# Seeding a partial sum from ScalarE, and folding the 64-channel rest into the seven products: 49 matmuls a chunk for 50

## The chip, the core and the metric

The kernel runs on one core of a Trainium2 chip. Its engines are named as the profile names them: PE is TensorE (matmuls; PEld is its weight load), DVE is VectorE, ACT is ScalarE, POOL is GpSimd, SP is SyncE, which here only issues transfers. Each engine takes its own instructions in the order built, and waits for others through semaphores. The metric is the device time of one execution in microseconds (us); the median of three runs of the kernel before is 1569.44 us.

## What is computed

One pre-norm transformer block over x of 2048 tokens by 576 channels, in fp32. The second half, the gated MLP, matters here:

```python
h = x + _A_ref(_layernorm(x, axis=-1), A_wqkv, A_wo)       # sliding dilated attention, 32 heads
...
g = jnp.einsum("bsd,df->bsf", x, w_gate)                   # x is _layernorm(h); D 576, F 4608
u = jnp.einsum("bsd,df->bsf", x, w_up)
h = _sigmoid(g) * u
return jnp.einsum("bsf,fd->bsd", h, w_down)
```

## The kernel before

**Precision.** A product in fp32 is made of three fp32r passes: each operand is split into a high part (ACT copies and rounds it) and a low part (DVE subtracts the high part), and high x high, high x low and low x high are accumulated in PSUM. `split` (L104 on ACT, L105 on DVE) does this for all operands.

**Channels.** Of the 576 input channels 512 are four slabs of 128; the last 64, the rest, lie twice on 128 partitions (high part above, low part below), so that two matmuls (`rest`, L754) make its three passes.

**Tokens and chunks.** The 2048 tokens are four blocks of 512. F is worked in 36 chunks of 128. The program's loop over `c` has 84 items: 12 plain chunks on block 0 (`single`), 24 paired chunks on blocks 0 and 1 (`pair`), 12 plain chunks that give block 1 its first third of F, and 36 paired chunks on blocks 2 and 3, the last pair (c from 48 on). Attention of the later blocks, its output projection, and the preparation of the next pair's operands run as background generators (`under_first`, `under_rest`) under these chunks.

**A paired chunk** multiplies a 2 by 2 block matrix of activations (a00 and a01: two pairs of channel slabs of one block; a10, a11 of the other) with a 2 by 2 block of weights (gate and up) in Strassen-Winograd form: seven products (weights b00, b10, t2, t3, t1, t4, b11; operands a00, a01, s2, s3, s1, a11, s4) of two slabs in three passes, so six matmuls each (`prod`, L747), and four rests of two matmuls: 50 matmuls of 128x128 by 512. The products accumulate in three PSUM banks, `b_tile`: b1 takes b00, then t2, then t1, then b11, and is copied out or added between them; b2 takes b10; b3 takes t3 and t4. Sums of banks are made by copying a bank to an `s` tile (ACT: L824, L834, L838), adding another bank to it (DVE: L829, L843, L848), then a sigmoid (ACT: L830, L849) and the gating product (DVE).

```python
        prod(b1, X["a00"], w, "b00", True)
        act.activation(s1, b1, AF.Copy)
        prod(b2, X["a01"], w, "b10", True)
        added[0] = dve.tensor_tensor(s1, s1, b2, ALU.add)
        act.activation(s1, s1, AF.Sigmoid)
```

`turn` rotates the banks by one from chunk to chunk. A plain chunk has its gate in the first bank and its up half in the second.

**The down product.** Between the products stand small units of down-projection matmuls (128x128 by 288, six to a unit in the last pair, PSUM tile `dp`, two buffers). In the last pair they are in the same seven-product form over two chunks (`seven`, `down_seven`): 14 units for two chunks, in each half k = 0 to 6 in two buffers, where k = 0, 2, 4, 6 accumulate in one buffer and 1, 3 and 5 in the other. After each unit ACT copies the buffer to an `ev` tile (L936; two units to a tile, four tiles), and POOL issues an accumulating DMA of it to DRAM (L939).

**Weights.** SP loads a chunk's weights two chunks ahead (`wg`, 640 KB in the last pair). `weights` makes the sums t1 to t4 in a tile `tw` (DVE, L727, L728, L730) and splits all into w1 (two buffers), w2, w3 and w4 (one buffer each). 

**Order.** A list scheduler sets each engine's order from priorities (`high_priority`: 700 for what empties banks, 400 for weights and operand splits) and from its own estimate of when things are ready.

## Time and profile before

| | |
|---|---|
| median of three runs | 1569.44 us (1568.37 to 1570.96) |
| span of the profiled execution, first to last instruction | 1566.1 us |
| PE, PEld busy | 1545.8 us (99%), 1374.2 us (88%) |
| DVE, ACT, POOL busy | 1254.3 us (80%), 882.6 us (56%), 207.4 us (13%) |
| granted TensorE clock | 1.000 |
| the last pair (936.6 us to the end) | 629.5 us |

The profile lists one execution, whose span is 3.3 us shorter than the median of the timed runs; a run's time has a little around the span. Busy shares are means over stages with different limits, so the stages are looked at one by one: attention with the first projections up to 219 us, the first plain chunks up to 350 us, the first pair up to 773.6 us, the second row of plain chunks up to 936.6 us, the last pair from there. In a group's row stand line, engine, operation, tiles, count, then busy time, mean ns of one, and idle time before. In the rows of windows stand the window, its length, busy us of PE, PEld, DVE, ACT, POOL with counts, clock, DMA share and GB/s.

### The profile page before, as it was taken

The page shows a single profiled execution, that of the slowest core. Times are in us where ns is not written, and L with a number is a line of the kernel's source. Part 1 is how long each engine was busy: PE and PEld are TensorE (multiplying, and loading weights), DVE is VectorE, ACT ScalarE, POOL GpSimd, SP SyncE. Part 2 cuts the span into 40 slices and gives each one's busy share as a digit, 9 for nine tenths or more (in the row PEclk, how much of TensorE's full clock was granted, in tenths as well). Part 3 has the DMA queues.
Part 4 walks back from the last instruction along what each step waited for, and adds up shares of the span by engine and source line. Part 5 has one row for each costly group of instructions (what it writes and reads, how often), then busy time and mean ns, then how long its engine had stood idle before and what let it go on. Part 6 is the DMA issues. An engine that isn't in the chain of part 4 may idle for free.

```text
span 1566.1 us, 22356 instructions
## 1 busy us (share of the span) xinstructions
PE 1545.8 (99%) x8520; PEld 1374.2 (88%) x8520; DVE 1254.3 (80%) x1880; ACT 882.6 (56%) x1584; POOL 207.4 (13%) x252
## 2 busy tenths in 40 slices
PE   8999999999999999999999999999999999999998
PEld 7999988887888888888888988888888888888888
DVE  7998999979999999999536688866777776677754
ACT  6632344435566555665542355766777666677761
POOL 3300000011000010000101000121112112112212
PEclk9999999999999999999999999999999999999999
DMA  8646555366565775665683424998899989989983
GB/s 281 219 166 222 190 200 183 107 225 199 145 174 150 200 183 150 162 159 125 180 243 113 179 85 119 205 180 176 170 181 186 172 172 183 175 170 181 185 166 137
DMA packets 77148, 273.96 MB, mean 175 GB/s; under 512 B 8336, under 2 KB 14224, under 8 KB 76144
## 3 DMA queue, kind: packets, MB, share of 16 engines
q0 software_dynamic: 28192, 107.29, 37.4%
q1 hardware_dynamic: 41216, 145.11, 27.8%
q10 hardware_dynamic: 7632, 20.12, 3.3%
q8 instruction: 66, 1.08, 0.3%
q14 instruction: 42, 0.34, 0.1%
HBM read 143.98 MB, written 130.87 MB: 176 GB/s over the span
## 4 chain that ended last, share of the span: by engine, by line
PE 82%; DVE 10%; DMA 5%; ACT 2%; issue 1%; POOL 0%; SPq 0%; ACTq 0%; POOLq 0%; DVEq 0%
PE b L747 40%; PE dp L868 14%; PE dp L930 11%; PE b L754 8%; PE acc L157 4%; DMA wg<-in_wmlp_dram 2%; DVE pr L189 2%; DVE lg L193 1%; DVE pr L215 1%; PE b L157 1%; PE bgp L157 1%; DMA x<-tok 1%; DVE w L105 1%; DMA kw<-k 1%; DVE pr L221 1%
## 5 line engine op out<-in xcount | busy, mean ns | idle before, releaser
L747 PE MATMUL b<-tl,w 128*128 128x512 f32 x1692 | 429.6, 393 | 1.2 <-ACT s L824 0.6
L747 PEld LDWEIGHTS b<-tl,w 128*128 128x128 f32 x1692 | 305.8, 188 | 57.9 <-ACT tl L104 1.2
L747 PE MATMUL b<-th,w 128*128 128x512 f32 x1332 | 343.0, 392 | 0.5 <-DVE s L843 0.5
L747 PEld LDWEIGHTS b<-th,w 128*128 128x128 f32 x1332 | 242.7, 188 | 45.3 <-DVE s L843 0.9
L936 ACT ACTIVATE ev<-dp 128x576 f32<-128x576 f32 x224 | 145.0, 647 | 62.9 <-PE dp L930 58.6
L754 PE MATMUL b<-th,w 128*128 128x512 f32 x564 | 174.9, 391 | 0.0
L939 POOL DMA_DIRECT2D h<-ev x128 | 109.2, 853 | 459.4 <-ACT ev L936 445.6
L104 ACT ACTIVATE w<-wg 128x384 fp32r<-128x384 f32 (+1 forms) x186 | 111.0, 600 | 98.5 <-PE b L754 54.4
L157 PE MATMUL acc<-qw,th 128*128 128x432 f32 x512 | 154.5, 363 | 2.4 <-DVE th L109 2.3
L105 DVE TENSOR_TENSOR w<-wg,w 128x384 fp32r<-128x384 f32 (+1 forms) x186 | 121.0, 656 | 36.7 <-ACT w L104 36.5
L105 DVE TENSOR_TENSOR w<-tw,w 128x512 fp32r<-128x512 f32 x120 | 82.6, 688 | 81.6 <-ACT w L104 80.7
L754 PEld LDWEIGHTS b<-th,w 128*128 128x128 f32 x564 | 106.0, 188 | 23.0
L868 PE MATMUL dp<-d,h1h 128*128 128x288 f32 x640 | 118.8, 295 | 0.0
L868 PE MATMUL dp<-d,h0h 128*128 128x288 f32 x608 | 112.2, 295 | 0.0
L876 ACT ACTIVATE stage<-dp 128x576 f32<-128x576 f32 x104 | 66.9, 646 | 68.1 <-PE dp L868 67.8
L157 PEld LDWEIGHTS acc<-qw,th 128*128 128x128 f32 x512 | 96.9, 189 | 7.7 <-DVE th L109 3.1
L868 PEld LDWEIGHTS dp<-d,h1h 128*128 128x128 f32 x640 | 98.7, 189 | 3.0
L868 PEld LDWEIGHTS dp<-d,h0h 128*128 128x128 f32 x608 | 94.0, 189 | 3.5 <-DVE stage L878 0.3
L104 ACT ACTIVATE w<-tw 128x512 fp32r<-128x512 f32 x120 | 75.3, 628 | 35.7 <-PE b L747 34.6
L157 PE MATMUL acc<-qw,tl 128*128 128x432 f32 x256 | 92.8, 363 | 0.1
L189 DVE TENSOR_TENSOR pr<-kw,q 128x2304 f32<-128x2304 f32 x32 | 81.8, 2555 | 8.3 <-DMA kw<-k 8.1
L884 POOL DMA_DIRECT2D h<-stage x26 | 31.1, 1197 | 416.2 <-ACT stage L876 337.2
(323 smaller groups left out, 2969.6 us busy)
## 6 DMA issues: line engine op xcount, KB each, us to landing
h<-ev POOLq DMA_DIRECT2D x96, 576.0 KB, 7.3
wg<-in_wmlp_dram SPq DMA_DIRECT2D x47, 928.0 KB, 5.2
h<-stage POOLq DMA_DIRECT2D x26, 1152.0 KB, 11.6
wg<-in_wmlp_dram SPq DMA_DIRECT2D x36, 640.0 KB, 4.2
kw<-k SPq DMA_DIRECT2D x16, 792.0 KB, 4.6
vw<-v SPq DMA_DIRECT2D x16, 792.0 KB, 4.9
wd<-in_wmlp_dram SPq DMA_DIRECT2D x18, 576.0 KB, 7.2
h<-ev POOLq DMA_DIRECT2D x32, 288.0 KB, 6.8
```

What stands on the lines that cost most here:

```text
L104: act.activation(hi, src, AF.Copy)
L105: splits.append(dve.tensor_tensor(lo, src, f32(hi), ALU.subtract))
L157: pe.matmul(ps[:, :n], a[:, c, js], m[:, c], start=k == 0, stop=False)
L189: dve.tensor_tensor(pr, both(kw, u), q[:, us].unsqueeze(2).broadcast_to([P, 2, W, CG]), ALU.mult)
L747: pe.matmul(ps, wt[:, a, k0 + c], xx[:, m + c], start=first and k == 0, stop=k == 5, skip_group_check=True)
L754: pe.matmul(ps, wt[:, a, k0], xx[:, 4], start=False, stop=a == 1, skip_group_check=True)
L868: pe.matmul(ps[:, i, :DH2], a[:, js], d[:, m, i * DH2:(i + 1) * DH2], start=k == 0, stop=k == n)
L876: act.activation(hv, ps, AF.Copy)
L884: pool.dma_start(hacc[b], hs, accum_op=ALU.add, max_dma_last_dim=8 * D)
L930: pe.matmul(ps[:, i, :DH2], a[x][:, js], m[y], start=k in (0, 1, 3) and q == 0, stop=q == 2, skip_group_check=True)
L936: act.activation(hs[:, k % 2], ps[:, :, :DH2], AF.Copy)
L939: pool.dma_start(hsev[:, u, k0:k + 1], hs[:, :k + 1 - k0], accum_op=ALU.add, max_dma_last_dim=8 * D)
```

## The change

**Seeding.** In `pair`, from the second chunk of a row on, ACT copies the first product from its bank into the bank of b10 (PSUM to PSUM) rather than to s1, b10 accumulates on it, and the sigmoid reads the bank: the DVE sum L829 goes. The products' order becomes b00, t3, t2, b10, t1, t4, b11. The banks no longer rotate: the first two swap from chunk to chunk, the third stays with t3 and t4. At the start of a row the first bank is the second one of `b_tile`, in which the plain chunk before has its up half. The gating product of the second block is issued ahead of b11.

**Rest in the products.** For the last pair the rest is halved into 32 channels for each column block of operands and laid out on four 32-partition quarters: operand high, low, high, low against weight high, high, low, low. One matmul makes all passes, and the halves take part in the seven sums: 7 x 7 = 49 matmuls. For this, `proj_scr` writes the raw rest of blocks 2 and 3 to DRAM, 16 POOL transfers read it back fourfold, `sums_rest` adds four DVE sums, and `split_quads` splits each of the seven operands with one ACT copy and two DVE subtractions, where three operands had one subtraction. The weights come from another array (768 KB a chunk for 640), are summed in place in `wg` after b00, b10 and b11 have been split from it, and take 10 DVE and 5 ACT instructions for 7 and 4.

**Space.** `s` has 3 buffers for 4, `ev` 3 for 4, `d3` 1 for 2.

```diff
+
+    def split_quads(t, src):
+        act.activation(t, src, AF.Copy)
+        for q in (32, 96):
+            dve.tensor_tensor(t[q:q + 32], src[q:q + 32], f32(t[q:q + 32]), ALU.subtract)
...
-        dve.tensor_tensor(rd, a0[:, 4], a1[:, 4], ALU.subtract)
-        yield
+        if rd is not None:
+            dve.tensor_tensor(rd, a0[:, 4], a1[:, 4], ALU.subtract)
+            yield
+    def sums_rest(q0, q1, s1):
+        (a00, a01), (a10, a11) = q0, q1
+        dve.tensor_tensor(s1, a10, a11, ALU.add)
+        yield
+        dve.tensor_tensor(a10, a00, a10, ALU.subtract)
+        yield
+        dve.tensor_tensor(a00, s1, a00, ALU.subtract)
+        yield
+        dve.tensor_tensor(a01, a01, a00, ALU.subtract)
+        yield
+        return dict(s1=s1, s2=a00, s3=a10, s4=a01, a11=a11)
+
+
+    def x_full(n, raw, rest):
+        if n in ("a01", "a11", "s4"):
+            t = th_tile()
+            r = t[:, 4]
+        else:
+            t = tl_tile()
+            r = xr.tile([P, TB], F32R, name="x" + n)
+        split(t[:, 0:2], t[:, 2:4], raw)
+        split_quads(r, rest)
+        XR[n] = r
+        return t
+
+    XR = {}
+    xr = None
...
-    def weights(kind, ws, down):
+    def full_weights(ws):
+        r = ws[:, :GF].rearrange("p (b c n) -> p b c n", b=4, c=3)
+        r1 = r.rearrange("p b c n -> p (b c) n")
+
+        def quads(t, src):
+            act.activation(t, src, AF.Copy)
+            dve.tensor_tensor(t[64:128], src[64:128], f32(t[64:128]), ALU.subtract)
+
+        with tc.high_priority(HI):
+            w1 = gw.tile([P, 2, 5, P], F32R, bufs=2, name="w1")
+            act.activation(w1[:, :, 0:3], r[:, 2:4], AF.Copy)
+            dve.tensor_tensor(w1[:, :, 3:5], r[:, 2:4, 1:3], f32(w1[:, :, 1:3]), ALU.subtract)
+            dve.tensor_tensor(w1[64:128, :, 0], r[64:128, 2:4, 0], f32(w1[64:128, :, 0]),
+                              ALU.subtract)
+            w4 = gw.tile([P, 6, P], F32R, name="w4")
+            act.activation(w4[:, 0:3], r[:, 0], AF.Copy)
+            dve.tensor_tensor(w4[:, 3:5], r[:, 0, 1:3], f32(w4[:, 1:3]), ALU.subtract)
+            dve.tensor_tensor(w4[64:128, 0], r[64:128, 0, 0], f32(w4[64:128, 0]), ALU.subtract)
+            dve.tensor_tensor(r1[:, 0:6], r1[:, 0:6], r1[:, 3:9], ALU.subtract)
+            dve.tensor_tensor(r[:, 2], r[:, 0], r[:, 2], ALU.add)
+            dve.tensor_tensor(r[:, 3], r[:, 3], r[:, 2], ALU.subtract)
+            ts = []
+            for name, b in (("w2", 0), ("w3", 2)):
+                t = gw.tile([P, 2, 4, P], F32R, name=name)
+                split(t[:, :, 0:2], t[:, :, 2:4], r[:, b:b + 2, 1:3])
+                ts += [t[:, 0], t[:, 1]]
+            tr = gw.tile([P, 8, P], F32R, tag="tw", name="tr")
+            quads(tr[:, 0:4], r[:, :, 0])
+        ww = {n: (t[:, 1:5], t[:, 0]) for n, t in
+              (("b00", w1[:, 0]), ("b10", w1[:, 1]), ("b11", w4))}
+        ww.update({n: (t, tr[:, i]) for i, (n, t) in enumerate(zip(("t3", "t1", "t2", "t4"), ts))})
+        return ww, None
+
+    def weights(kind, ws):
...
         k = 0
         for c in range(2):
             for a, m in ((0, 0), (0, 2), (1, 0)):
-                pe.matmul(ps, wt[:, a, k0 + c], xx[:, m + c], start=first and k == 0,
+                lhs = wt[:, a, k0 + c] if isinstance(k0, int) else wt[:, 2 * a + c]
+                pe.matmul(ps, lhs, xx[:, m + c], start=first and k == 0,
                           stop=k == 5, skip_group_check=True)
                 k += 1
+
+    def product(ps, n, xn, w, first, rests):
+        prod(ps, X[xn], w, n, first)
+        if isinstance(w[n][1], int):
+            for m, wn in rests:
+                rest(ps, X[m], w, wn)
+        else:
+            pe.matmul(ps, w[n][1], XR[xn], start=False, stop=True, skip_group_check=True)
 
     def rest(ps, xx, w, n):
         wt, k0 = w[n]
...
-        return gh.tile([P, TB], F32, tag="s", bufs=4, name="s")
+        return gh.tile([P, TB], F32, tag="s", bufs=3, name="s")
...
     added = [None]
     gated = [None]
 
-    turn = [2]
-
-    def pair(X, w, between, last):
-        turn[0] += 1
-        b1, b2, b3 = (b_tile(turn[0] + k) for k in range(3))
+    order = [1, 0, 2]
+
+    def pair(w, between, last):
+        n1, n2, n3 = order[:3]
+        clean = order[3:]
+        order[:] = [n2, n1, n3, True]
+        b1, b3, b2 = b_tile(n1), b_tile(n3), b_tile(n2)
         s1, s2, s3 = s_tile(), s_tile(), s_tile()
-        prod(b1, X["a00"], w, "b00", True)
+        product(b1, "b00", "a00", w, True, ())
         with tc.high_priority(HC):
-            act.activation(s1, b1, AF.Copy)
+            act.activation(b2 if clean else s1, b1, AF.Copy)
         between(0)
-        prod(b2, X["a01"], w, "b10", True)
-        rest(b2, X["a01"], w, "g4")
+        product(b3, "t3", "s3", w, True, ())
         with tc.high_priority(HC):
-            added[0] = dve.tensor_tensor(s1, s1, b2, ALU.add)
-            act.activation(s1, s1, AF.Sigmoid)
+            act.activation(s3, b3, AF.Copy)
         between(1)
-        prod(b1, X["s2"], w, "t2", False)
+        product(b1, "t2", "s2", w, False, ())
         with tc.high_priority(HC):
             act.activation(s2, b1, AF.Copy)
         between(2)
-        prod(b3, X["s3"], w, "t3", True)
+        product(b2, "b10", "a01", w, not clean, (("a01", "g4"),))
         with tc.high_priority(HC):
-            act.activation(s3, b3, AF.Copy)
+            if clean:
+                act.activation(s1, b2, AF.Sigmoid)
+            else:
+                dve.tensor_tensor(s1, s1, b2, ALU.add)
+                act.activation(s1, s1, AF.Sigmoid)
         between(3)
-        prod(b1, X["s1"], w, "t1", False)
-        rest(b1, X["a11"], w, "u4")
+        product(b1, "t1", "s1", w, False, (("a11", "u4"),))
         with tc.high_priority(HC):
             added[0] = dve.tensor_tensor(s3, s3, b1, ALU.add)
         between(4)
-        prod(b3, X["a11"], w, "t4", False)
-        rest(b3, X["a11"], w, "g4")
+        product(b3, "t4", "a11", w, False, (("a11", "g4"),))
         with tc.high_priority(HC):
             added[0] = dve.tensor_tensor(s2, s2, b3, ALU.add)
             gated[0] = act.activation(s2, s2, AF.Sigmoid)
         between(5)
-        prod(b1, X["s4"], w, "b11", False)
-        rest(b1, X["s4"], w, "u4")
         with tc.high_priority(HC):
-            last((s1, b1), (s2, s3))
+            last(1, s2, s3)
+        product(b1, "b11", "s4", w, False, (("s4", "u4"),))
+        with tc.high_priority(HC):
+            last(0, s1, b1)
         between(6)
 
     tails = {}
...
-                    hs = st.tile([P, 2, 2, DH2], F32, bufs=4, name="ev")
+                    hs = st.tile([P, 2, 2, DH2], F32, bufs=3, name="ev")
...
+        elif b > 1:
+            pool.dma_start(rscr[b - 2], raw[0:DR, 4])
...
         s = [pp.tile([P, 2, TB], F32, name=f"rs{i}") for i in range(3)]
         rd = pp.tile([P, TB], F32, name="rd")
         if p == 1:
+            rr = [[pp.tile([P, TB], F32, name=f"rr{i}{h}") for h in range(2)] for i in range(2)]
+            for i in range(2):
+                for h in range(2):
+                    a = rscr[i][32 * h:32 * h + 32, :]
+                    for q in range(4):
+                        pool.dma_start(rr[i][h][32 * q:32 * q + 32], a)
+                    yield
             for n in ("a00", "a01"):
                 a = a0[:, 0:2] if n == "a00" else a0[:, 2:4]
                 with tc.high_priority(HI):
-                    Xn[n] = x_half(a, None if n == "a00" else a0[:, 4])
+                    Xn[n] = x_full(n, a, rr[0][n == "a01"])
                 yield
-        raw = yield from sums(a0, a1, a1[:, 0:2] if p == 1 else a0[:, 0:2], *s, rd)
+            raw = yield from sums(a0, a1, a1[:, 0:2], *s, None)
+            rq = yield from sums_rest(*rr, rd)
+            raw = {n: (raw[n][0], rq[n]) for n in rq}
+            for n in names:
+                with tc.high_priority(HI):
+                    Xn[n] = x_full(n, *raw[n])
+                yield
+            return raw
+        raw = yield from sums(a0, a1, a0[:, 0:2], *s, rd)
         for n in names:
             with tc.high_priority(HI):
                 Xn[n] = x_half(*raw[n])
...
+        if c in (NSTD, NF + NSTD):
+            del order[3:]
-                    Xn[n] = x_half(*raw[n])
+                    Xn[n] = x_full(n, *raw[n])
-            wc = weights(items[c + 1][0], wg, c + 1 < NF + NSTD)
+            wc = (full_weights(wg) if c + 1 >= NF + NSTD else
+                  weights(items[c + 1][0], wg))
-            wg = load_gu(items[c + 2][2], n=WC if c + 2 < NF + NSTD else GU)
+            wg = load_gu(items[c + 2][2], c + 2 >= NF + NSTD)
-        def last(h0, h1):
-            hid[0] = hidden(*h0, "h0")
-            hid[1] = hidden(*h1, "h1")
+        def last(t, sg, ps):
+            hid[t] = hidden(sg, ps, f"h{t}")
...
```

What this does to the order is shown at three places; b1 to b3 are the three banks, `dp` the down units, w1 to w4 weights, `tr` the rests of the weights (new), `xa..`, `xs..` those of the operands (new).

PE, end of the first chunk of the last pair (c = 48), before: t1 and its rest, t4, b11, then the next chunk's b00 and b10, t2, t3, then the first unit of the down products (h0).

```order
L747 MATMUL b2_9212<-tl_9019,w3_9036 128x512 x6
L754 MATMUL b2_9212<-th_9022,w4_9034 128x512 x2
L747 MATMUL b1_9214<-th_9022,w3_9036 128x512 x6
L754 MATMUL b1_9214<-th_9022,w1_9031 128x512 x2
L747 MATMUL b2_9212<-th_8904,w4_9034 128x512 x6
L754 MATMUL b2_9212<-th_8904,w4_9034 128x512 x2
L747 MATMUL b3_9345<-tl_8832,w1_9194 128x512 x6
L747 MATMUL b1_9346<-th_8835,w1_9194 128x512 x6
L754 MATMUL b1_9346<-th_8835,w1_9194 128x512 x2
L747 MATMUL b3_9345<-tl_8892,w2_9198 128x512 x6
L747 MATMUL b2_9347<-tl_8895,w2_9198 128x512 x6
L930 MATMUL dp_9382<-d_9230,h0h_9188 128x288
```

The same place now: the next chunk's b00 has moved up ahead of t4, its rest matmul is the first row; t1 stands behind t4, b11 directly behind t1, and the first matmul of the h0 unit directly behind b11.

```order
L825 MATMUL b1_9249<-xa00_8860,w1_9061 128x512
L825 MATMUL b3_9084<-xs3_8985,tr_8954 128x512
L815 MATMUL b3_9084<-th_9051,w3_8951 128x512 x6
L825 MATMUL b3_9084<-th_9051,tr_8954 128x512
L825 MATMUL b2_9083<-xs2_8968,tr_8954 128x512
L815 MATMUL b2_9083<-tl_9044,w2_8948 128x512 x6
L825 MATMUL b2_9083<-xs1_9045,tr_8954 128x512
L815 MATMUL b2_9083<-th_8991,w4_8941 128x512 x6
L825 MATMUL b2_9083<-th_8991,w4_8941 128x512
L1009 MATMUL dp_9422<-d_9268,h0h_9223 128x288
L815 MATMUL b2_9251<-th_8876,w1_9061 128x512 x5
L815 MATMUL b3_9250<-tl_8984,w2_9072 128x512 x2
```

PE in the steady part of the last pair, around the units s1, h1 and s4 (the fifth to the seventh of a half), before: between any two units stands a product.

```order
L930 MATMUL dp<-d,s1h 128x288 x2
L930 MATMUL dp<-d,s1l 128x288
L930 MATMUL dp<-d,s1h 128x288
L747 MATMUL b_12066<-th,w_11854 128x512 x6
L754 MATMUL b_12066<-th,w_11854 128x512 x2
L930 MATMUL dp<-d,h1h 128x288
L930 MATMUL dp<-d,h1l 128x288
L930 MATMUL dp<-d,h1h 128x288 x2
L930 MATMUL dp<-d,h1l 128x288
L930 MATMUL dp<-d,h1h 128x288
L747 MATMUL b_12065<-tl,w_11858 128x512 x6
L930 MATMUL dp<-d_11552,s4h 128x288
```

Now s1, h1 and s4 follow each other between b00 and t3, with nothing between.

```order
L1009 MATMUL dp<-d,s1h 128x288 x2
L1009 MATMUL dp<-d,s1l 128x288
L1009 MATMUL dp<-d,s1h 128x288
L1009 MATMUL dp<-d,h1h 128x288
L1009 MATMUL dp<-d,h1l 128x288
L1009 MATMUL dp<-d,h1h 128x288 x2
L1009 MATMUL dp<-d,h1l 128x288
L1009 MATMUL dp<-d,h1h 128x288
L1009 MATMUL dp<-d_11965,s4h 128x288
L1009 MATMUL dp<-d_11965,s4l 128x288
L1009 MATMUL dp<-d_11965,s4h 128x288 x2
L815 MATMUL b_12484<-tl,w_12277 128x512 x2
```

DVE in the steady part, from the gating product behind b11 (its bank as input) on, before: w4's split (384 wide), and the sums L728 and L730 in their own tile `tw`, which do not wait for it.

```order
L1187 TENSOR_TENSOR r_12180<-s,b_12065 128x512
L105 TENSOR_TENSOR w_12050<-wg,w_12050 128x384
L728 TENSOR_TENSOR tw<-wg,tw 128x256
L105 TENSOR_TENSOR h0l<-r_12180,h0h 128x512
L730 TENSOR_TENSOR tw<-wg,tw 128x256
L829 TENSOR_TENSOR s<-s,b_12216 128x512
L105 TENSOR_TENSOR w_12201<-tw,w_12201 128x512
L843 TENSOR_TENSOR s<-s,b_12215 128x512
```

Now the split of w4 (L764, L765), whose single buffer b11 was the last to read, the three in-place sums (L766 to L768) and the splits of w2, w3 and the rests stand in one row behind it, all of them for the next chunk's t3 and t2.

```order
L1285 TENSOR_TENSOR r_9821<-s,b_9706 128x512
L764 TENSOR_TENSOR w_9688<-wg,w_9688 128x256
L765 TENSOR_TENSOR w_9688<-wg,w_9688 64x128
L1276 TENSOR_TENSOR wd<-wd 128x288
L107 TENSOR_TENSOR h0l<-r_9821,h0h 128x512
L766 TENSOR_TENSOR wg<-wg 128x768
L767 TENSOR_TENSOR wg<-wg 128x384
L768 TENSOR_TENSOR wg<-wg 128x384
L107 TENSOR_TENSOR w_9695<-wg,w_9695 128x2x256
L107 TENSOR_TENSOR w_9698<-wg,w_9698 128x2x256
L754 TENSOR_TENSOR tr<-wg,tr 64x512
L922 TENSOR_TENSOR s<-s,b_9859 128x512
```

46 lines of the change are left out of this document (27 added, 19 removed).

## The prediction

> **What bounds the kernel now.** I read the shares first, then windows by stage, then the groups and the row of single instructions in the stage that the change is for.
>
> ```profile
> PE 1545.8 (99%) x8520; PEld 1374.2 (88%) x8520; DVE 1254.3 (80%) x1880; ACT 882.6 (56%) x1584; POOL 207.4 (13%) x252
> core 0: us, PE busy (x) PEld busy (x) DVE busy (x) ACT busy (x) POOL busy (x), PEclk, DMA share, GB/s
> 400.50:773.60 373.10, 373.07 (x2060) 330.61 (x2060) 350.39 (x441) 220.28 (x360) 32.73 (x31) 1.00 0.64 162
> 905.00:936.60 31.60, 31.60 (x180) 27.85 (x179) 26.96 (x41) 18.76 (x33) 0.99 (x1) 1.00 0.24 82
> 936.60:985.00 48.40, 48.40 (x250) 41.80 (x248) 43.10 (x76) 27.48 (x50) 2.99 (x3) 1.00 0.52 131
> 954.40:965.75 11.35, 11.35 (x51) 9.38 (x50) 11.11 (x22) 7.46 (x15) 0.00 (x0) 1.00 0.56 135
> 1031.70:1510.80 479.10, 479.10 (x2577) 418.66 (x2577) 346.38 (x599) 341.74 (x602) 95.51 (x112) 1.00 0.91 177
> ```
>
> PE is the bound, and in the windows from 400.5 us on it is as good as never idle. The last row is 28 chunks of 50 + 42 matmuls (28 x 92 = 2576): 479.1 / 28 = 17.11 us a chunk, with DVE at 72% and ACT at 71%. 954.40 to 965.75 is the second chunk of the last pair, in which no down unit stands: its 50 matmuls take 11.35 us, 0.227 us each. So a matmul less is worth 0.227 us only as long as PE stays fed, and everything hangs on what the new order makes PE wait for. At the start of the last pair (905 to 985) DVE has only 31.60 - 26.96 + 48.40 - 43.10 = 9.9 us left.
>
> **The change part by part.** *Fewer matmuls.* 36 chunks lose one each: 36 x 0.227 = **-8.2 us**, all on PE's path. The stacked matmul has the 128x512 shape of the others. [...]
>
> *Weights and operands.* The rows that give the prices:
>
> ```profile
> L727 DVE TENSOR_TENSOR tw<-wg 128x512 f32<-128x512 f32 x28 | 19.3, 688 | 0.0
> L728 DVE TENSOR_TENSOR tw<-wg,tw 128x256 f32<-128x256 f32 x28 | 11.8, 420 | 0.0
> L105 DVE TENSOR_TENSOR w<-wg,w 128x640 fp32r<-128x640 f32 x28 | 23.0, 820 | 0.0
> L105 DVE TENSOR_TENSOR w<-wg,w 128x384 fp32r<-128x384 f32 x28 | 15.5, 553 | 0.0
> L829 DVE TENSOR_TENSOR s<-s,b 128x512 f32<-128x512 f32 x28 | 19.3, 688 | 25.9 <-PE b L754 25.3
> L936 ACT ACTIVATE ev<-dp 128x576 f32<-128x576 f32 x196 | 126.8, 647 | 53.5 <-PE dp L930 49.6
> L104 ACT ACTIVATE w<-wg 128x640 fp32r<-128x640 f32 x28 | 20.2, 723 | 0.0
> L824 ACT ACTIVATE s<-b 128x512 f32<-128x512 f32 x28 | 16.6, 593 | 2.8 <-PE b L747 2.7
> ```
>
> Seven DVE instructions (820, 553, two of 689 for w2 and w3, 688, 420, 420) make 4.28 us a chunk now; ten of widths 128 to 768, at 0.15 + 0.00105 us per column (the line through 420 and 688), make about 5.9. Less the seeded sum's 0.69 that is +1.0 us a chunk on DVE and, with two copies of 256 and 512 columns, 0.8 on ACT: 72 and 71% become some 78 and 76%. Nothing by itself; it uses up margins that I price below.
>
> *Loads, stores, buffers.* SP's weight load grows from 640 to 768 KB.
>
> ```profile
> q0 software_dynamic: 13791, 49.40, 71.8%
> q1 hardware_dynamic: 6720, 22.81, 18.9%
> h<-ev POOLq DMA_DIRECT2D x72, 576.0 KB, 7.4
> wg<-in_wmlp_dram SPq DMA_DIRECT2D x24, 640.0 KB, 4.7
> ```
>
> A load of 4.7 us becomes about 5.6, issued two chunks (34 us) ahead: hidden. `ev` with three buffers: a tile is filled in 2.4 + 0.65 us, stored in 7.4, so busy 10.8 us; three tiles serve 7 units in 17.1 us, so one comes round in 3 x 2 x 17.1 / 7 = 14.7 us at an even pitch, some 12 in the uneven one: hidden by a thin margin (the third rival). The 16 POOL reads of 64 KB and the two writes fall between attention and 936 us, where the DMA share is 0.24 to 0.64; of POOL's queue only stores stand behind them: 0 (0 to 1). One buffer less for `s` and `d3`: the third `s` tile of a chunk is free after its gating product, a chunk early: 0.
>
> *Steady wait at the down units.* In the new order the units s1, h1, s4 stand in one row; s1 and s4 share a `dp` buffer, so s4 may start only when ACT has copied s1's sum, with h1 alone as cover.
>
> ```profile
> 1201.99 0.30 PE L930 MATMUL dp<-d,s3h 128*128 128x288 f32 x1
> 1202.78 1.55 PE L747 MATMUL b<-tl,w 128*128 128x512 f32 x6
> 1214.48 0.30 PE L930 MATMUL dp<-d,h0h 128*128 128x288 f32 x1
> 1214.81 0.65 ACT L936 ACTIVATE ev<-dp 128x576 f32<-128x576 f32 x1 [1.26 <-PE dp L930]
> 385.71 1.20 PE L747 MATMUL b<-tl,w 128*128 128x512 f32 x4 [0.57 <-ACT s L824]
> ```
>
> The first two rows are a unit's first matmul and what follows the unit: 0.79 us for six (0.132 each). The next two are a unit's last matmul and its copy: the matmul ends 0.17 us after the next could start, 0.03 later ACT starts and takes 0.65, some 0.04 back: 0.89 us, 0.10 more than h1 covers. The last row shows what a wait costs beyond itself: four matmuls after one take 1.20 us where four at 0.227 with the modelled tail of 0.17 make 1.07: about 0.11. So 0.21 a chunk x 33 = **+6.9 us**. Between 0 (ACT quicker, the units spread) and 0.7 a chunk, 23 us (ACT is within another copy of 0.65 us when s1 ends). I take the near end, since ACT waits 1.26 us for PE in the row above. [...] In the row of 385.71 PE did idle 0.57 us.
>
> *Steady chain at the weights.* Now the next chunk's splits of w4, the three in-place sums, and the splits of w2, w3 and the rests stand on DVE behind the gating product of b11, since w4 has one buffer and the sums overwrite what w4 is split from; before, the sums wrote `tw`. By the widths: the gating product 0.69, w4 0.42 + 0.29, a down weight's sum 0.46, h0's split 0.69, the sums 0.95 + 0.55 + 0.55, w2's split 0.69, together 5.3; less 0.08 for each of eight that follow directly (936.61 + 0.68 against 937.21, in the table below), and 0.3 for handoffs: 4.9 us. PE has as cover b00 (7 x 0.227 = 1.6), the three units (2.4) with their wait (0.2), and the first four of t3's passes, which need no low part of w2 (0.9 to 1): about 5.2. It fits by 0.3 us, less than one ACT copy of 0.65 that may stand ahead of a split on ACT. I take half the chunks late by a quarter of a microsecond: 0.13 x 33 = **+4.3 us** (0 to 0.6 a chunk, 20 us).
>
> *Start of the last pair.* The rows before and at 936.6 us, DVE first:
>
> ```profile
> 932.89 1.22 DVE L105 TENSOR_TENSOR th<-rs,th 128x1024 fp32r<-128x1024 f32 x1
> 934.14 0.69 DVE L109 TENSOR_TENSOR th<-rd,th 64x512 fp32r<-64x512 f32 x1
> 934.87 0.69 DVE L105 TENSOR_TENSOR w<-tw,w 128x512 fp32r<-128x512 f32 x1
> 935.47 1.22 DVE L105 TENSOR_TENSOR tl<-rs,tl 128x1024 fp32r<-128x1024 f32 x1
> 936.61 0.68 DVE L767 TENSOR_TENSOR s<-s,b 128x512 f32<-128x512 f32 x1
> 937.21 0.75 DVE L878 TENSOR_TENSOR stage<-stage,dp 128x576 f32<-128x576 f32 x1
> 936.64 1.54 PE L747 MATMUL b<-tl,w 128*128 128x512 f32 x6
> ```
>
> DVE has no gap here, and gets, by `split_quads` and `sums_rest`, 14 subtractions and sums of 512 columns more than before (11 and 3; some 0.60 us from start to start, as 936.61 to 937.21): 8.4 us, and the weights of three chunks, 3 x 1.4, less two seeded sums, 1.2: 11.4 us into 9.9 of idle time, so 1.5 us at least and more by order. The first product now takes the second bank; the gating product at 936.61, which reads it, ends at 937.29, while b00 starts at 936.64: with handoff and restart 0.8 us, and 2.2 with DVE's added work ahead of it. In chunk 48 no unit and no free product stands between t2's copy and t1 (0.17 + 0.03 + 0.60 + 0.04 + 0.11 = 0.95), between t1's sum and b11 (0.69 for 0.60: 1.04), between b11 and the h0 unit (product 0.69, copy 0.62, handoffs: 1.75), and t4 waits for its operand or the copy of t3 (0.95 to 2). That is 4.7 to 5.8. Chunks 49 and 50 repeat two such handoffs each (2.7). Together 2.2 + 5.3 + 2.7 and some 1 of DVE's surplus: **+11 us** (4, if only DVE's surplus and the bank count, to 15, all of these and DVE's 1.5 in full behind the operands).
>
> *Start of the first pair.* The same bank change, where DVE had more room; there is no added operand: **+1** (0 to 2). *Seeding inside the pairs.* A sum less on DVE (25.9 us of waiting ahead of L829 in the table above belonged to DVE, not PE), the copy's shape stays 128x512 from PSUM; that it writes PSUM no row before shows. I take 0.593, and if it were twice that, t3 and t2, 3.2 us between it and b10, would still hide it: 0; should b10 follow it directly, it would be 0.95 a chunk.
>
> Sum: -8.2 + 6.9 + 4.3 + 11 + 1 = **+15 us**. The profiled execution's span of 1566.1 would be 1581, and the median, 3.3 above it, 1569.4 + 15 = 1584.4, say **1585 us**.
>
> **The rivals.** *The saving comes whole* (other side): the scheduler's waits find cover. It decides at s4: if the copy of s1 and its handoffs take under 0.79 us, as they would with one matmul more between, and the weights' chain keeps its 0.3 us of margin, 11.2 us go; if the operands are ready at 936 us, 11 more. Then 1569.4 - 8.2 = 1561 us. For it: ACT and DVE idle over a fifth of the steady time. Against it: the three units in one row, and in-order engines.
> *Only the start costs.* Steady chunks at 16.9 us, the 11 + 1 us of the starts paid by the 8.2: 1573 in full, 1569 with starts of 8.
> *Stores run late.* With a DMA share of 0.91 going to about 0.94 and three `ev` tiles, an ACT copy waits for a store, holds `dp`, and so PE: 0.3 to 1 us a chunk on top, 10 to 33 us: about 1600 and above. For it: 10.8 of 12 us; against it: stores land in 7.4 us at a share of 0.91 already.
>
> **How the numbers follow.** Forecast 0.72, saving whole 0.12, only the start 0.06, stores late 0.10. A change of 0.2% (3.1 us) is about what can be told from none. Faster is the first rival, 0.12; same the second, 0.06; slower the rest, 0.82. The forecast's bounds, not all at one end at once, are +1 (a start of 4 and half the steady waits) to +33; I cut the top at +33 and leave out the first rival below, 0.12, and about 0.08 above: 1570 to 1602.
>
> **What would show it.** Right: 8484 matmuls; steady chunks of 17.1 to 17.3 us and not 16.9; PE waits on `dp` for ACT's copy to `ev`, some 0.1 to 0.2 us a chunk, and on t3 for the rests of w; 936 to 985 us longer by about 10 us, with PE idle there and `b` waiting for DVE's gating product at 936. Wrong: no PE idle from 985 us on; PE waits for `ev` that end with a DMA; b10's wait for the seeding copy in every chunk; matmuls that are not 0.227 us apart.

## The result, and the profile after

The changed kernel takes 1664.8 us (median of 4 runs) against 1569.7: 1.060 times as long, 95% interval 1.058 to 1.062. The forecast was 1585 us, in a range of 1570 to 1602. The direction was right, and 63 us above the range were not foreseen. The profiled execution has a span of 1668.4 us, 102.3 more than before; the page of the kernel after, and the windows that were shown of the kernel before:

```profile
PE 1584.7 (95%) x8484; PEld 1381.1 (83%) x8484; DVE 1305.0 (78%) x1944; ACT 904.1 (54%) x1624; POOL 218.9 (13%) x270
core 0: us, PE busy (x) PEld busy (x) DVE busy (x) ACT busy (x) POOL busy (x), PEclk, DMA share, GB/s
400.50:773.60 373.10, 373.10 (x2062) 330.89 (x2062) 336.33 (x421) 220.80 (x360) 32.69 (x31) 1.00 0.65 162
905.00:936.60 31.60, 31.60 (x178) 27.75 (x178) 25.52 (x41) 16.57 (x30) 10.02 (x20) 1.00 0.42 128
936.60:985.00 48.40, 40.88 (x173) 31.59 (x173) 39.30 (x63) 21.08 (x35) 1.27 (x1) 0.86 0.30 82
1031.70:1510.80 479.10, 441.70 (x2251) 370.71 (x2249) 340.62 (x584) 313.66 (x557) 84.52 (x99) 0.98 0.83 167
```

The 36 matmuls are gone (8484), and the first pair is as it was. In the steady window PE issues 2251 matmuls where it issued 2577, 91 to a chunk: 19.37 us a chunk for 17.11. PE is idle 37 us of that window, and the granted clock, 1.00 in every window before, is 0.98, at the start of the last pair 0.86. DVE and ACT are less busy than I had worked out, 71 and 65%: they are not full, they wait.

From the starts of chunks 36, 48, 51 and 82 in PE's rows come the lengths of the stages (us, profiled executions; before chunk 36 little of the edits is at work, the seeding and one `s` buffer less, and the executions differ by some us there). The rows below the first two are experiments and are told further down.

```
                        to c 36   36-48   48-51   51-82   82-end   span    a chunk 51-82
before                   773.6    163.0    43.7   530.5    55.3   1566.1   17.11
after                    775.8    165.5    60.5   598.7    67.9   1668.4   19.31
seedonly                 778.1    164.3    44.6   529.4    55.3   1571.7   17.08
restonly                 777.5    164.5    60.5   577.3    69.8   1649.6   18.62
pin                      777.9    165.9    65.2   636.4    62.6   1708.0   20.53
late                     777.0    165.7    56.8   542.4    57.6   1599.5   17.49
w4two                    774.9    164.6    53.0   525.8    58.5   1576.8   16.96
w4rest                   779.1    165.8    56.0   523.0    57.9   1581.8   16.87
w4rm3dk                  775.4    168.8    46.5   522.6    58.0   1571.3   16.86
```

So of 102 us, 68 lie in the 31 steady chunks, 17 in the three before them, 13 at the end (where 10.2 us ran at half the clock). The waits of the last pair (936 to 1600 us; engine, tile and line, who was waited for, us in total, times, longest):

```profile
ACT w L758 <- DMA wg<-in_wfull_dram: 84.3, 33, 4.1
PE dp L1009 <- ACT ev L1015: 36.5, 34, 1.7
PE b L815 <- ACT w L106: 8.7, 14, 0.8
```

PE's first wait is the one forecast, s4 for the copy of s1, but 1.07 us each time, not 0.10. The first row is new, and was not in the prediction at all: ACT stands 2.55 us a chunk at the copy that makes w1, for the weight load. One chunk, in order of time (DVE's last reader of a wg buffer; SP's next load into it; ACT at the copy to w1; then PE from h1's last matmul):

```profile
1203.33 0.69 DVE L754 TENSOR_TENSOR tr<-wg,tr 64x512 fp32r<-64x512 f32 x1 [0.37 <-ACT tr L753]
1204.04 21.23 SPq L738 DMA_DIRECT2D wg<-in_wfull_dram  x2
1211.16 0.84 ACT L758 ACTIVATE w<-wg 128x768 fp32r<-128x768 f32 x1 [3.00 <-DMA wg<-in_wfull_dram]
1217.71 0.29 PE L1009 MATMUL dp<-d,h1h 128*128 128x288 f32 x1
1219.73 0.44 PE L1009 MATMUL dp<-d,s4h 128*128 128x288 f32 x1 [1.72 <-ACT ev L1015]
1219.96 0.44 PE L1009 MATMUL dp<-d,s4l 128*128 128x288 f32 x1
1220.20 0.68 PE L1009 MATMUL dp<-d,s4h 128*128 128x288 f32 x2
1220.68 1.05 PE L815 MATMUL b<-tl,w 128*128 128x512 f32 x2
wg<-in_wfull_dram SPq DMA_DIRECT2D x21, 768.0 KB, 7.1
```

The buffer is given back at 1204.02, when the low parts of the rests have been made from it; the load is issued 0.02 us later and lands after 7.1 us. ACT is at the copy at 1208.16 and stands 3.00 us, with all of its later copies behind it. The load and the copy serve chunk 63, which PE starts at 1235.04. In the kernel before, the last reader of the buffer was the split of w4, and the same copy came 13.4 us after the load's issue; the last row is PE's start of the chunk that they serve:

```profile
1202.80 0.55 DVE L105 TENSOR_TENSOR w<-wg,w 128x384 fp32r<-128x384 f32 x1
1203.38 0.33 SPq L702 DMA_DIRECT2D wg<-in_wmlp_dram  x1
1216.73 0.72 ACT L104 ACTIVATE w<-wg 128x640 fp32r<-128x640 f32 x1
1237.01 0.39 PE L747 MATMUL b<-tl,w 128*128 128x512 f32 x1
```

So both loads are issued more than 30 us ahead of PE's use (31.0 and 33.6). What is short is the stretch to their first reader, ACT's copy, which the scheduler puts more than a chunk ahead of that use. The median over chunks 54 to 81:

| us | before | after |
|---|---|---|
| load issued, after the start of the chunk two before its own | 0.8 | 9.1 |
| load issued, ahead of its own chunk | 33.4 | 29.7 |
| copy to w1 started, ahead of its own chunk | 20.3 | 22.6 |
| from the load's issue until ACT is at the copy | 13.1 | 4.6 |

The rows of PE behind the wait show the second thing: the 288-matmuls stand 0.24 us apart, not 0.13, and the 512-matmuls 0.43, not 0.227. This window of the kernel after has its clock (eighth field: PEclk):

```profile
1219.73:1222.50 2.77, 2.77 (x10) 2.48 (x11) 2.77 (x6) 1.71 (x4) 0.86 (x1) 0.54 0.99 176
```

### The profile page after: what moved, and what is told of

It reads as the page before. It is cut to its first block, busy times and chain, and to the rows that moved or that the text cites. A ratio compares the mean times of both kernels' runs of the same rounds, so it can differ in the third digit from the quotient of the medians.

```text
span 1668.4 us, 22305 instructions
## 1 busy us (share of the span) xinstructions
PE 1584.7 (95%) x8484; PEld 1381.1 (83%) x8484; DVE 1305.0 (78%) x1944; ACT 904.1 (54%) x1624; POOL 218.9 (13%) x270
## 5 line engine op out<-in xcount | busy, mean ns | idle before, releaser
L815 PE MATMUL b<-tl,w 128*128 128x512 f32 x1692 | 456.5, 402 | 18.8 <-ACT w L106 12.7
L815 PEld LDWEIGHTS b<-tl,w 128*128 128x128 f32 x1692 | 311.2, 192 | 88.6 <-ACT w L106 21.0
L815 PE MATMUL b<-th,w 128*128 128x512 f32 x1332 | 360.3, 397 | 2.3 <-ACT s L906 1.4
L815 PEld LDWEIGHTS b<-th,w 128*128 128x128 f32 x1332 | 246.5, 190 | 51.1 <-ACT s L906 2.6
L106 ACT ACTIVATE w<-wg 128x384 fp32r<-128x384 f32 (+2 forms) x186 | 111.4, 601 | 101.7 <-PE b L830 34.0
L107 DVE TENSOR_TENSOR w<-wg,w 128x384 fp32r<-128x384 f32 (+2 forms) x186 | 123.6, 668 | 43.6 <-ACT w L106 43.3
L922 DVE TENSOR_TENSOR s<-s,b 128x512 f32<-128x512 f32 x60 | 41.0, 684 | 94.6 <-PE b L825 89.9
L830 PE MATMUL b<-th,w 128*128 128x512 f32 x276 | 85.7, 390 | 0.0
L222 DVE TENSOR_TENSOR pr<-vw,lg 128x2304 f32<-128x2304 f32 x32 | 81.8, 2557 | 0.8
L200 DVE TENSOR_REDUCE lg<-pr 128x128 f32<-128x2304 f32 x32 | 81.6, 2549 | 0.3
```

Source lines behind the costliest of these rows:

```text
L106: act.activation(hi, src, AF.Copy)
L107: splits.append(dve.tensor_tensor(lo, src, f32(hi), ALU.subtract))
L200: dve.tensor_reduce(lg[:, us].rearrange("p j w h -> p (j w h)"), pr.rearrange("p j w (h d) -> p (j w h) d", d=DH), AX.X, ALU.add)
L222: dve.tensor_tensor(pr.rearrange("p j w (h d) -> p j w h d", d=DH), both(vw, u).rearrange("p j w (h d) -> p j w h d", d=DH), lg[:, us].uns ...
L815: pe.matmul(ps, lhs, xx[:, m + c], start=first and k == 0, stop=k == 5, skip_group_check=True)
L830: pe.matmul(ps, wt[:, a, k0], xx[:, 4], start=False, stop=a == 1, skip_group_check=True)
```

## The experiments

Times are medians; each is compared with runs of the kernel before on the same chip (1571.1 to 1571.9 us), and "+" is the difference to those.

**Is it the load? (late)** The edit holds ACT's copy back, so that the load has most of a chunk, and has all of the next chunk's weight work stand in the program behind the first product:

```diff
-            act.activation(w1[:, :, 0:3], r[:, 2:4], AF.Copy)
+            with tc.issue_after(seeded[0]):          # the seeding copy of the chunk before its use
+                act.activation(w1[:, :, 0:3], r[:, 2:4], AF.Copy)
...
+                if i == 0 and c + 1 < len(items):    # in between(0), not ahead of the chunk
+                    wc = full_weights(wg_here)
```

> The changed kernel, but the next chunk's weights are emitted after the chunk's first product, and the ACT copy that makes the high parts of b00 and b10 (w1) is held back until the seeding copy of that chunk; the load it reads has then been under way for most of a chunk. Theory L (the load): the sums in place keep a wg buffer busy until the split of the rests, the load then lands 5.4 to 7.1 us later, ACT stands 84.3 us in all (33 times 2.55) at the copy to w1, and every later copy on ACT comes late, s1's copy to ev above all. L expects ACT's wait for the load to go from 84 to under 5 us, PE's wait for the copy to ev from 36.5 to under 12 us, steady chunks of 17.1 instead of 19.3 us: about 1664.8 - 33 x 2.2 = 1592 us (1582 to 1608). Theory U (the units): what counts is that s1, h1 and s4 stand in one row; ACT's wait only lies beside it. U expects the wait for ev to stay near 30 us and the time above 1640 us.

Measured: 1601.5 us, +29.6 (1.019, 1.017 to 1.021), for +95.2: the load theory's number. No wait of ACT for the load is left. The steady window and PE's remaining wait in it:

```profile
1031.70:1510.80 479.10, 475.39 (x2495) 404.57 (x2494) 366.57 (x640) 348.62 (x613) 94.09 (x110) 1.00 0.90 182
PE dp L1013 <- ACT ev L1019: 3.5, 14, 0.2
```

The load took as long as before the edit (7.1 us), it only wasn't waited for. The three units still stand together, with at most a few of t3's matmuls among them, so the row is not what costs 1.07 us; with ACT on time PE waits there 0.25 us every second chunk.

**Is it the three units? (pin, latepin)** One unit behind each product, alone and with the edit above:

```diff
+        with pin():        # tc.issue_after(the last matmul before), around each product and each unit
             prod(ps, X[xn], w, n, first)
```

> The changed kernel with PE's order in the last pair fixed as written: one unit of the down products behind each product, so a product of 1.6 us stands between s1 and h1 and between h1 and s4. Theory U expects PE's 36.5 us of waiting for the copy to ev to go, and with it the half-speed matmuls behind those waits: 1664.8 - 36 - 20 = about 1610 us. Theory L expects ACT to stand as long at the load as now (over 60 us), the wait for ev to be replaced by waits for w copies and for other banks, and 1625 to 1665 us.

> Both edits together: the copy to w1 held back, and one unit behind each product. L and U both expect steady chunks of 16.9 to 17.0 us with PE hardly idle; what is left is the start of the last pair, about 25 us by the trace of the changed kernel (936 to 1002 us), and the tail: 1569.7 - 8.2 + 25 = 1586 us (1562 to 1595). If it stays above 1610 us there is a third cause in the steady part, DVE's or ACT's load.

Measured: 1712.8 us (+140.9) and 1759.1 (+187.3). Both theories missed. pin shows why (waits in the steady window):

```profile
PE b L834 <- DVE tr L754: 24.6, 24, 1.8
PE b L823 <- ACT w L106: 22.7, 24, 1.5
PE b L823 <- DVE w L107: 9.2, 24, 0.6
```

All three rows are waits inside t3, the second product of the chunk, for its weights: 2.4 us a chunk. The row of three units was not the cause of a wait but the cover of another: the next chunk's weights come late, and with the units between the products nothing hides that. In latepin the same waits are 2.5 us a chunk, and its mean clock is 0.951. So there was a third cause in the steady part, as the expectation of latepin allowed, but it is neither DVE nor ACT being full (61 and 58% busy there in the steady window): the waits name the weights' lateness.

**Which part of the change? (restonly, seedonly)** The two halves of the change, each alone: the stacked rest with the old order of products and banks; and the kernel before with seeding, new order and fixed banks.

```diff
# restonly, against after: pair() as in the kernel before
-        product(b3, "t3", "s3", w, True, ())
+        product(b2, "b10", "a01", w, True, (("a01", "g4"),))
...
# seedonly, against before: pair() as in the kernel after, rests, weights and buffers untouched
-            act.activation(s1, b1, AF.Copy)
+            act.activation(b2 if clean else s1, b1, AF.Copy)
```

> The changed kernel with the pair's order, bank rotation and DVE sum of the kernel before (no seeding), but with the rest stacked into the seven products: 49 matmuls a chunk, weights summed in place. Theory L puts the loss on the weights' part alone: ACT's wait for the load stays above 50 us, and the time is well above before, 1610 to 1660 us, though b10 now stands between s1 and h1 and may hide part of it. Theory U (the new order of products brings the three units together) expects 1565 to 1585 us.

> The kernel before with the first part of the change alone: seeding, the new order of products, the fixed banks; rests, weights and buffers as before, 50 matmuls a chunk. PE was never idle in the steady part before, so a DVE sum less brings nothing there: steady chunks 17.11 us. What it can cost are the starts of the two pairs (the bank, about 1.3 us each): 1569.7 + 2.6 = 1572 us (1569 to 1576). If the new order of products were the cause of the loss, it would be above 1590 us here too.

Measured: restonly 1651.4 (+79.5), seedonly 1573.0 (+1.9; 1.0017, 1.0003 to 1.0031), as expected. The loss comes with the stacked rest and not with the seeding. That half holds the weights, the operands and the smaller buffers; which of them it is, this pair of runs does not say. In restonly ACT's wait for the load is still 58.3 us in all.

**Does the landing decide? (split2)**

```diff
+        if full:                          # b00 and b10 first, 384 KB, then the other half
+            sp.dma_start(ws[:, n // 2:n], src[f][:, n // 2:n])
+            n //= 2
         behind[0] = sp.dma_start(ws[:, :n], src[f][:, :n])
```

> The changed kernel, but each weight load of the last pair is issued as two transfers of 384 KB, first the half with b00 and b10, which ACT's copy to w1 reads, then the other; nothing on ACT, DVE or PE is asked to move. Theory L (ACT stands at the copy to w1 because the load lands 5.4 to 7.1 us after the buffer is given back): the first half lands in about 3.5 to 4 us, ACT's wait of 84 us falls below 25 us, PE's wait for the copy to ev from 36 to about 12 us, the time to about 1610 us (1595 to 1625). Rival: the gain of the run with the copy held back came from the copy's new place in ACT's row, not from the load; then this run stays above 1645 us.

Measured: 1640.3 (+69.2), too slow for the load theory's number, and under the rival's bound of 1645 by too little to decide alone. Its trace tells why (a DMA group, with median us to landing; and ACT's wait from 936 to 1600 us):

```profile
wg<-in_wfull_dram SPq DMA_DIRECT2D x44, 384.0 KB, 6.3
ACT w L761 <- DMA wg<-in_wfull_dram: 68.0, 32, 4.4
```

The first row is the median of both halves. Apart, the first landed 6.2 us after its issue, not 3.5, and the second, issued 0.37 us behind it, after 6.7: they overlapped. The edit took 16 us from the wait and 26 from the time; it did not do what it was for, and leaves open by itself whether the load or the copy's place counts.

**The root (w4two).** Why are the weights late, and why is the buffer given back late? In the order of DVE shown above, the sums in place stand behind the split of w4, and that behind b11, the last reader of the one w4. The ring of w1 has room for a second:

```diff
-            w4 = gw.tile([P, 6, P], F32R, name="w4")
+            if c % 2:
+                w4 = gw.tile([P, 6, P], F32R, name="w4")
+            else:
+                w4 = gw.tile([P, 2, 5, P], F32R, tag="w1", bufs=2, name="w1")
+                w4 = w4.rearrange("p a n q -> p (a n) q")[:, 0:6]
...
-            del order[3:]
+            order[:] = [0, 1, 2]          # latebank: this edit alone, on late
```

> As the run with the copy to w1 held back, but each row of pairs starts with its first product in the first bank, as in the kernel before, not in the bank that the last plain chunk's gating product still reads. The bank theory expects the wait of 1.06 us ahead of chunk 48's first product, with its restart, and some 1 us at the start of the first pair to go: 1601.5 - 2.5 = 1599 us (1597 to 1601). If DVE hands the operands over late anyway, the wait only moves behind that product: 1601 to 1603 us.

> The changed kernel with one tile more for the weights of b11: w4 of every other chunk goes into the ring of w1, which has room for it, so that the next chunk's w4 can be split while b11 still reads the old one; pairs start in the first bank, as in the run that gave 1599.2 us. ACT's copy to w1 is not held back. Theory W: the single w4 is the root. The sums in place wait for w4's split and so for b11; that makes the weights of t3 late (hence s1, h1, s4 in one row), and gives the wg buffer back late (hence the wait for the load). W expects all three to go: ACT's wait for the load under 5 us, PE's wait for the copy to ev under 3 us, steady chunks of 16.9 to 17.0 us, and only the start of the last pair left: 1599.2 - 31 x 0.55 = 1582 us (1574 to 1587). If DVE and ACT are simply too full with 49 matmuls a chunk, steady chunks stay at 17.4 or above and the time at 1597 us or more.

Measured: latebank 1599.2 (+28.1), w4two 1581.3 (+9.7; 1.0066, 1.0047 to 1.0085). In the steady window PE is never idle, at full clock, and no wait for the load or for ev is left there:

```profile
1031.70:1510.80 479.10, 479.10 (x2577) 416.65 (x2577) 376.00 (x659) 360.47 (x636) 98.03 (x114) 1.00 0.91 188
```

2577 matmuls as before, now 91 to a chunk: 16.96 us. The scheduler by itself put a unit behind each product again. DVE at 78% and ACT at 75% were not too full.

The edit moved both ends of the short stretch. The load is issued 1.5 us into the chunk two before its own (9.1 in the kernel after), so the buffer does come back early. ACT's copy also moved, to 12.4 us ahead of its chunk for 22.6, since w4 now takes turns in the ring of w1. The first alone would have been enough: a copy 22.6 us ahead would have stood 9.8 us behind the issue, and the load landed after 5.5 us (median) here. That is worked out from the medians; no run has the early load with the copy left in its place.

**The same without seeding (w4rest):** restonly with the edit of two w4 tiles.

> The run without seeding (1651.4 us: old order of products and banks, rest stacked into the seven products) with two tiles for w4. Theory W expects the same cure without the seeding: steady chunks of 16.9 to 17.1 us and 1575 to 1588 us. If the seeding is needed for it (DVE has 0.69 us more a chunk here), it stays above 1595 us.

Measured: 1578.6 (+6.9; 1.0040, 1.0025 to 1.0055), 16.87 us a chunk: the whole saving of 0.227, without the seeding. What is left lies ahead of the steady chunks, most of it in chunk 48, and 2.6 us at the end.

**The start: is it DVE? (latepool, w4nolow, w4more)**

```diff
-            dve.tensor_tensor(t[q:q + 32], ...)     # split_quads, sums_rest
+            pool.tensor_tensor(t[q:q + 32], ...)    # latepool, on late
                                                     # w4nolow, on w4two: split_quads' line left out
+        if c >= NF + 4 and i in (1, 4):             # w4more, on w4two: in twice()
+            bg_step(i)
```

> As the run with the copy to w1 held back (1601.5 us), and the 14 subtractions of the operands' rests and the four sums of rests go to POOL, which is idle in that stage: DVE gets 18 instructions (about 10.8 us) less around 925 to 965 us. If DVE's surplus at the start of the last pair is what delays the operands, the three chunks from c = 48 take 10 us less (56.8 to 47) and the time is about 1591 us. If the handoffs inside chunk 48 are what costs, nothing moves: 1598 to 1604 us; slower if POOL's own instructions come later than DVE's did.

> As the run with two tiles for w4, but the 14 subtractions that make the low parts of the operands' rests are left out (the rests then enter with their high parts alone): 14 x 0.6 = 8.4 us of DVE less at the start of the last pair. DVE theory: the three chunks from c = 48 get 6 to 9 us shorter. Handoff theory: under 2 us shorter.

> As the run with two tiles for w4, and the background work that prepares the last pair's operands is stepped twice more per plain chunk from the fifth chunk of the row on, so that it starts its splits earlier, while DVE is half idle. If DVE's surplus around 936 us is what costs at the start, the three chunks from c = 48 (57 us, 43.7 before) get 6 to 10 us shorter, and the time is 1572 to 1576 us. If the handoffs inside chunk 48 cost, it stays within 2 us of the run it is built on.

Measured: latepool 1609.6, 8 us slower than late; w4nolow 1582.0 and w4more 1583.9, within 2.5 us of w4two. latepool says little on DVE, since POOL takes 1.6 us for what DVE did in 0.69:

```profile
944.43 6.24 POOL L116 TENSOR_TENSOR xs<-rr,xs 32x512 fp32r<-32x512 f32 x4
```

w4nolow, which leaves out the low parts of the operands' rests and so computes something else, is of more use: chunk 48 took 19.1 us instead of 25.1, and chunk 49 18.9 instead of 12.7. DVE's surplus did cost 6 us, and something else took its place. The trace of w4nolow, DVE, in chunk 49:

```profile
966.17 0.69 DVE L1287 TENSOR_TENSOR r<-s 128x512 f32<-128x512 f32 x1 [3.79 <-DMA h<-stage]
```

The first tile of the hidden values lies where the plain chunks' last results are still being stored. In the kernel before this instruction waits for no DMA.

**The start cured as far as it went (w4restmore, w4restmore2, w4more2, w4rm2dk, w4rm3dk).** Background steps added from the fifth plain chunk on (w4restmore, on w4rest), or at every place from the third (w4restmore2 and w4rm2dk on w4rest, w4more2 on w4two) or the sixth (w4rm3dk, on w4rest); and, in the last two, the tile moved:

```diff
+        if phase is not ATT and c >= NF + 2:        # w4rm3dk: NF + 5
+            bg_step(i)
...
-                    for n in ("s4h", "s4l", "s1h"):
+                    for n in ("s4h", "s4l", "s1h", "s1l", "s3l", "s3h", "s2l"):
```

> The run without seeding and with two tiles for w4 (1578.6 us, steady chunks 16.87 us), with the background work stepped twice more per plain chunk from the fifth chunk of the second row on. There PE stands 5.7 us for the low parts of the operands' rests at the start of the last pair, and the clock is 0.90 there. If the late operands are the cost of the start, the three chunks from c = 48 (56.0 us, 43.7 before) take 45 to 49 us and the time is 1568 to 1572 us, level with the kernel before or a little under it. If the handoffs of chunk 48 cost whatever the operands do, it stays at 1576 to 1580 us.

> The same with one background step more at every place of the plain chunks from the third on, so that the operands are ready several chunks ahead: operand theory 43 to 46 us for the three chunks and 1564 to 1570 us; handoff theory 1576 to 1580 us. If the earlier steps push other work of the row aside, the row itself (163 us before) gets longer by what is saved.

> The changed kernel with seeding, two tiles for w4, pairs starting in the first bank, and the same early background steps: operand theory 1564 to 1572 us. If the seeding itself costs at the start (its copy to b10's bank waits on ACT, 5.2 us in one run), it stays 4 to 8 us above the run without seeding.

> As the run without seeding, with two tiles for w4 and early background steps from the third plain chunk on (1580.7 us), but the tiles of the pool that holds the hidden values of the last pair are laid out so that its first one, r00, no longer lies where the last plain chunks' results are still being stored: DVE stood 3.5 us for that store, and PE 3.5 us behind it at the start of chunk 49, with half-speed matmuls after it. Expected: that wait gone, the three chunks from c = 48 43 to 47 us instead of 51, the time 1573 to 1576 us. If another wait takes its place, 1579 to 1581 us.

> The same, with the additional background steps only from the sixth plain chunk on, so that PE does not stand 5.2 us for the attention's output in the second row of plain chunks: 1567 to 1573 us, level with or under the kernel before (1571.1), if both the row and the start are then as in the kernel before and the 7 us of the steady part stay saved.

Measured: 1579.3 (+8.1), 1580.7 (+9.6), 1585.5 (+14.4), 1575.4 (+3.6) and 1574.3 (+2.5; 1.0014, 1.0002 to 1.0027). With early operands alone (the first three) the three chunks from 48 still took 52.2, 51.1 and 52.8 us, and the wait only moved, in w4restmore2 to the third product of chunk 49, where the store was waited for:

```profile
970.73 0.69 DVE L1283 TENSOR_TENSOR r<-s,b 128x512 f32<-128x512 f32 x1 [3.51 <-DMA h<-stage]
971.57 4.18 PE L819 MATMUL b<-tl,w 128*128 128x512 f32 x9 [3.52 <-DVE r L1283]
```

Nine matmuls in 4.18 us are 0.46 us each, for 0.227, and the granted clock from 936 to 985 us is 0.93. With the tile moved, three chunks from 48 take 45.0 and 46.5 us (43.7 before). The row of plain chunks then is 5 to 6 us longer, in w4rm2dk by PE's wait of 5.2 us for attention's output; w4rm3dk has only waits of 1.9 us and less there, and why its row is 168.8 us long stays open. w4more2, with seeding, is 4.8 us above w4restmore2, the size that was expected if the seeding costs something at the start; PE stood 4.5 us there for ACT's copy of t3's bank, and the cause was not isolated. No version beat the kernel before. In w4rm3dk the steady part saves 7.9 us, and the table says where they went, and 5.2 more: 5.8 in the row of plain chunks, 2.8 in chunks 48 to 50, 2.7 at the end, 1.8 ahead of chunk 36.

## Why the prediction was wrong, point by point

- **Loads "issued two chunks (34 us) ahead: hidden", 0 us.** This is the step that failed, by some 65 of the 95 us (after +95.2, late +29.6). The 34 us reach to PE's use of the weights, and 29.7 of them were there. But a load is hidden only if it lands ahead of its first reader, and that is ACT's copy, some 22 us ahead of PE's use. The load can be issued only when its buffer's last reader is done. I had quoted the sums in place and the split of the rests as DVE's row, and did not see that they now are that last reader: the issue came 8.3 us later into a chunk, and left 4.6 us to the copy where 13.1 had been. The landing was mis-sized too, 7.1 us for 5.6, but 5.6 would not have been hidden either. Had it been hidden, the forecast's range would have held the time, by its edge: late took 1601.5.
- **Restart, 0.11 us a wait.** Right for a wait of 0.91 us (some 0.1, last section), wrong for one of 1.72: behind it the clock was 0.54 over 2.77 us. In the kernel after, the granted clock is half for 47.8 us between its first and last matmul, which costs up to 24 us, an estimate (half of the 47.8); before, never. It follows on the first: without the load's wait, late has 6.8 us of it.
- **Down units, +6.9.** Place and mechanism were right, and the size too once ACT is on time: in late the gap ahead of s4 is 0.41 us longer than a unit's pitch, every second chunk, with 0.1 behind it, so 0.26 a chunk for 0.21. In the kernel after it is 36.5 us of idle PE: I had bounded ACT's lateness by one copy of 0.65 us, not by a load. PE's rows come in the order built, s4 behind h1 and t3's first two matmuls behind four of s4's: PE stood 1.72 us ahead of s4 at 1219.73, and t3 followed. That the row of units is the scheduler's answer to late weights I did not see; pin and w4two showed it.
- **Weights' chain, +4.3.** Right in place, half the size: from late to w4two a chunk falls from 17.49 to 16.96, 0.53 us, of which 0.26 are the units; 0.27 x 33 = 9 us. The place is seen in late's steady window, where PE's weight loads stood 5.9 us for ACT's copies of w and 5.1 for the rests' low parts.
- **Fewer matmuls, -8.2.** Right: w4rest has 16.87 for 17.11, and 0.227 us a matmul held.
- **Start of the last pair, +11.** The kernel after lost 2.5 + 16.8 us in the stages 36-48 and 48-51; without load and chain (w4two, first bank) 1.6 + 9.3, where the forecast without the bank's 2.2 is 8.8. The bank's share, by latebank, is 1.4 us at chunk 47's end (9.6 for 11.0); at the start of chunk 48 of the kernel after, PE stood 1.06 us for the gating product. The named handoffs were there: PE waited 0.91 and 1.29 us for the rests' low parts and 0.69 twice for a copy in w4two (PE's rows there, the bracket being the wait ahead). The store under the hidden values' tile was in no term.

```profile
956.71 0.47 PE L829 MATMUL b<-xs,tr 128*128 128x512 f32 x1 [0.91 <-DVE xs L116]
957.87 1.67 PE L819 MATMUL b<-th,w 128*128 128x512 f32 x6 [0.69 <-ACT s L910]
961.06 0.47 PE L829 MATMUL b<-xs,tr 128*128 128x512 f32 x1 [1.29 <-DVE xs L116]
962.23 1.66 PE L819 MATMUL b<-tl,w 128*128 128x512 f32 x6 [0.69 <-ACT s L914]
```

- **First pair, +1, and seeding, 0.** Right: chunks 12 to 36 took 423.6 us before and 424.9 after; seedonly costs 1.9 us in all, and the copy to PSUM took 0.58 us, for the 0.593 assumed.
- **The rivals.** "Stores run late" did not happen: no copy to ev waited for a DMA in the kernel after, and the stores landed after 5.8 us (median), not 7.4. The 10.8 us for a tile are 10.45 by the terms named (2.4 + 0.65 + 7.4). "The saving comes whole" is what the steady part does in w4rest, from another cause than the one named: the weights' buffer. The clock was in no rival and in no term. In the steady part I reckoned with waits of 0.1 to 0.25 us; late has waits of that size there and a clock of 1.00, the kernel after has waits of up to 1.7 us and 0.98.

## What to carry to other kernels

How far ahead a load really is is read from its buffer: find the buffer's last reader in the new order, add the landing time, and compare with the place of the first reader on its engine. A sum made in place ties three things together that were apart, the raw data's release, the split that must come first, and whoever holds that split's target; here a second place for w4, lent by the ring of w1, undid the knot. A strange order from a list scheduler (three units in a row) can be the cover of a wait and not its cause: here fixing the order by hand cost another 46 us.

## What the runs showed of the hardware

In the profile of the kernel after, the granted clock is half in ten spells between PE's first and last matmul: eight of 3.41 us, one of 6.83 and one of 13.65, together 47.8 us, with starts that lie whole multiples of 3.413 us apart. Ahead of each, PE had been idle, by the profile's modelled ends, for 1.71 to 2.42 us of the last 3.413. Of stretches of 3.413 us at the same spacing, 461 were at full clock and followed by full clock; in none of them was PE idle for more than 1.73 us. How the clock is set was not shown. A spell of 3.41 us at half speed costs up to 1.7 us, an estimate (half of it), beside the wait of 1.72 ahead of it at 1219.73. A wait of 0.91 us cost some 0.1: the clock from 1199.4 to 1202.8 us is 1.00, and the first matmul behind the wait is 0.40 us long, for 0.29 or 0.30 further on.

```profile
1199.49 0.40 PE L1009 MATMUL dp<-d,s4h 128*128 128x288 f32 x1 [0.91 <-ACT ev L1015]
```

Two transfers of 384 KB issued 0.37 us apart on the same queue landed after 6.2 and 6.7 us (medians), one of 768 KB after 7.1: splitting a load did not bring its first half early.
